# The last 16 rows of each head gathered in one transfer of 48 rows instead of three of 16, under a new list of steps

## The chip, the cores and the metric

One core of a Trainium2 chip runs the whole program. Its engines are TensorE (PE, matmuls; its weight loads are listed as PEld), VectorE (DVE), ScalarE (ACT), GpSimd (POOL) and SyncE (SP). Each works through its own queue in order. All transfers of this kernel are issued from SP's queue. The metric is device time in microseconds (us): the median of the runs before is 541.8 us, of three runs from 539.09 to 542.12.

## The reference

Two stages follow each other. The first is a gated linear recurrence for 4 batches and 8 heads over 768 steps, with head size 48:

```python
for t in range(S):
    state = alpha[:, :, t, :, None] * state + einsum('bhd,bhe->bhde', k[:, :, t], v[:, :, t])
    y[:, :, t] = einsum('bhd,bhde->bhe', q[:, :, t], state)
```

The second takes the 3072 tokens of width 384 that result through two layers with 2048 hidden units: `h = x @ w_in`, `g = h * erf(softplus(h))`, `out = g @ w_out`. All of it is float32.

## The kernel before, in words

The 768 steps are cut into 12 chunks of 64. For a chunk `n` the program has these steps, each a method of `Chunk`: `la`, `lk`, `lq`, `lv` load alpha, K, Q and v; `a1` makes the running product A of alpha (DVE); `ln` and `ex` its inverse (ACT); `w1`, `w2`, `w3` scale K with it and `a3` scales Q with A (DVE); `kx` and `qx` gather (below); `t` transposes K, `s` multiplies K by Q, `u` multiplies K by v into the state T, `q` multiplies Q by the old state and `y` adds the part from within the chunk (all PE), with copies on ACT or DVE behind them.

The second stage has 16 weight tiles for each layer. They arrive as 64-bit numbers and are turned into float32 and split into a high and a low half by the steps `wi_f` and `wo_f` (a load into `wst`, then six instructions on ACT and DVE). For chunk `n` the hidden units are done in four groups: `H_n_g_half` (first matmul, line 549; chunk 0 uses line 538 and the unsplit weights), `U`, `L1`, `G` (ACT tables and curves), `L2`, `Z` (DVE), `O_n_g` (split, then second matmul, line 617), and `out`.

**Layout and gather.** A head has 48 rows. Four head pairs stand in the tiles K and Q. Two halves of 64 partitions hold one head each, so that partitions 48 to 63 of each half would be empty. The fourth pair's 48 rows are loaded there: 16 of them behind each of the three first pairs (`KT` = 3). Before `s` and `q` can use the fourth pair, `last` (line 233) moves those 3 times 16 rows to 48 partitions of slot `KT`, in SBUF, for both halves. `kx` does it for K behind `w3`, `qx` for Q behind `a3`, and `ends` for the chunk's last column of A after every fourth chunk. Chunk 0 does its loads and products in two pieces (pairs 0 and 1, then the rest), and its gathers too.

**Order.** A written list, `SCHED`, of 1642 steps fixes the order on PE, ACT, DVE and SP: `steps()` takes the words one by one, and each engine gets its instructions in that order. A word `x` that stands several times is the step's next part each time; the prefix `v:` puts its copy on DVE instead of ACT. POOL holds a few small fills: the tail of `kn` in `t`, and a `token` behind each part of `q`, for which `y` waits. Large tiles share one pool of 24 buffers. In the compiled program each transfer waits on one of eight counters in turn, thus for the transfer issued eight before it.

Of the kernel before, what the change touches and what calls it, by code (L numbers as in the profile page):

```python
# [44 lines left out]
wi_15 wi_2 wi_7 wi_13 H_0_1_0 wi_15 wi_14 wi_3 v:wi_0 w2_2 lk_2 wi_13 wi_4 wi_12 wi_9 wi_15 wi_14 v:wi_12 wi_8 s_1
wi_3 s_1 wi_10 s_1 wi_2 wi_4 wi_1 H_0_0_1 w3_2 lv_1 H_0_0_1 H_0_2_0 wi_0 H_0_1_1 wo_9 wi_1 U_0_1 q_1 wo_7 wi_15 wi_0
t_1 wi_12 wi_1 wi_13 wo_9 v:wo_9 wi_12 v:wi_14 wo_7 wi_13 H_0_0_0 H_0_0_0 y_1 y_1 wi_0 wi_10 u_1 wi_3 wi_10 y_1 wi_11
wi_11 lq_2 wi_14 a3_2 wi_14 wi_6 wi_10 u_1 wo_9 H_0_2_0 wi_14 kx_2 v:y_1 U_0_0 la_3 v:wi_9 wo_2 H_0_3_1 wo_2 v:wo_2
a1_3 y_1 wo_9 L1_0_1 wo_13 t_2 wi_15 wi_13 wi_13 wo_1 wo_15 qx_2 wi_12 v:wi_11 wo_15 wo_0 v:wo_15 wi_14 H_0_3_1 y_1
H_0_3_0 wo_9 H_1_1_0 wi_11 s_2 wo_1 v:wo_1 t_2 wo_0 wi_12 lq_3 ln_3 wi_0 q_2 q_2 wi_11 wo_13 wo_3 t_2 wo_9 wo_15  # L50
H_1_1_0 wo_2 wo_2 wo_5 s_2 H_0_2_1 H_1_3_0 s_2 wi_11 wi_11 wo_15 wo_3 wo_1 v:wo_0 wi_9 wo_4 wi_10 wi_10 wi_15 H_0_2_1
wo_0 lv_2 ex_3 wo_15 w1_3 wo_15 v:wo_7 H_1_1_1 wo_7 H_1_3_0 wo_5 w2_3 H_1_0_1 wo_7 L1_0_1 wo_0 L1_0_0 H_1_1_0 y_2 wo_1
v:wo_3 u_2 wo_3 H_0_3_0 wo_0 y_2 a3_3 lk_3 w3_3 wo_4 wo_11 H_1_3_0 wo_7 wo_6 wo_13 v:wo_11 wo_1 L1_0_0 u_2 v:wo_4
H_1_2_1 lv_3 y_2 wo_13 H_1_0_0 y_2 H_2_0_0 wo_2 H_2_0_1 v:wo_11 H_1_1_1 L1_0_0 y_2 qx_3 L1_0_1 wo_13 wo_6 v:wo_6 wo_1
H_1_1_1 y_2 kx_3 U_0_3 wo_11 wo_4 H_1_0_1 L2_0_1 G_0_1 H_2_0_1 H_1_0_0 wo_2 wo_7 H_1_0_1 wo_3 wo_3 H_1_2_0 H_1_2_1
H_1_0_0 la_4 H_1_2_0 wo_4 H_2_0_0 L2_0_0 L2_0_0 G_0_0 L2_0_1 wo_0 H_2_0_0 H_1_2_1 wo_6 wo_13 H_1_2_0 q_3 la_6 H_2_0_1
v:wo_4 wo_3 s_3 s_3 s_3 Z_0_0 wo_4 Z_0_1 t_3 t_3 t_3 H_2_1_0 U_0_2 v:wo_5 wo_11 wo_5 q_3 L1_0_3 wo_14 u_3 gd_3 L1_0_3
wo_10 H_2_1_1 lq_4 y_3 wo_11 Z_0_0 O_0_0 H_1_3_1 u_3 H_2_2_1 wo_13 wo_6 wo_6 a1_4 H_1_3_1 H_2_2_1 L1_0_2 wo_11 H_2_2_1
ends_3 L1_0_3 wo_8 O_0_0 H_2_1_0 L1_0_2 y_3 y_3 y_3 wo_5 wo_10 H_2_2_0 L1_0_2 ln_4 Z_0_1 L2_0_3 L2_0_3 y_3 v:wo_8
# [10 lines left out]
Z_1_3 v:out_0_1 U_2_3 O_1_2 U_2_2 O_1_2 out_0_1 U_2_1 L1_2_1 H_3_3_0 qx_5 H_4_0_1 O_1_2 H_4_0_1 v:H_3_3_0 O_1_2  # L70
out_0_0 H_4_0_0 O_1_2 w3_5 H_4_2_1 L2_2_0 O_1_3 L1_2_1 H_4_2_0 L1_2_3 L1_2_1 v:H_4_0_1 H_3_3_1 kx_5 Z_2_0 L1_2_2 O_1_2
Z_2_0 t_5 t_5 t_5 O_1_3 q_5 q_5 H_3_3_1 O_1_3 v:H_4_0_0 lv_5 a1_6 H_3_3_1 s_5 L2_2_1 L2_2_1 O_2_0 L1_2_3 G_2_1 u_5 s_5
s_5 u_5 O_1_3 O_2_0 O_2_0 a1_7 L1_2_3 O_1_3 L1_2_2 y_5 y_5 O_2_0 y_5 Z_2_1 L1_3_0 O_1_3 L2_2_3 v:y_5 O_2_0 L1_2_2 ln_6
H_5_1_0 L1_3_1 Z_2_1 lk_6 O_2_0 ex_6 O_2_1 G_2_3 y_5 y_5 gd_6 L2_2_3 L2_2_2 O_2_1 H_4_3_0 G_2_2 w1_6 L2_2_2 O_2_1
Z_2_2 out_1_0 Z_2_3 Z_2_2 U_4_0 H_4_3_0 v:O_2_2 O_2_1 H_5_1_0 lq_6 H_4_1_0 L1_3_0 H_5_1_1 L1_3_0 H_4_3_1 out_1_0
H_5_1_1 out_1_1 out_1_1 w2_6 L2_3_0 L1_3_1 L1_3_1 H_4_1_0 H_5_1_1 w3_6 O_2_1 H_4_1_1 kx_6 O_2_1 L2_3_1 lv_6 a3_6 qx_6
H_4_3_1 v:H_5_1_0 L2_3_0 L1_4_0 H_4_1_0 G_3_1 O_2_2 O_2_2 v:H_4_3_0 v:H_4_3_1 H_4_1_1 H_4_1_1 gd_7 O_2_2 U_4_2 t_6
v:t_6 t_6 s_6 G_3_0 U_3_2 U_4_1 u_6 q_6 Z_2_3 O_2_2 O_2_3 s_6 H_5_2_1 Z_3_0 s_6 Z_3_0 U_3_3 q_6 L2_3_1 Z_3_1 L1_3_2
O_2_3 L1_4_1 O_2_2 L1_4_1 u_6 H_5_0_1 O_2_3 H_5_0_1 L1_4_0 O_2_3 L1_4_1 Z_3_1 H_5_0_1 O_3_1 y_6 y_6 y_6 y_6 L1_3_3
# [832 lines left out]
```

## Time and profile before

| | |
|---|---|
| median of 3 runs | 541.8 us (539.09 to 542.12) |
| profiled execution | 541.78 us, span 540.0 us |
| PE busy | 497.8 us |
| DVE busy | 467.5 us |
| ACT busy | 461.5 us |
| mean granted TensorE clock | 0.979 |
| transfers by `last` (line 236) | 72 for K, 72 for Q, 12 for `ends` |

The busy time counts instructions that overlap once. PE runs for 92% of the span, so the time is PE's work plus the places where PE stands still or runs at a lower clock; most of the reading is to find those places and what ended each.

### The profile page before, as it was taken

Reading aid. Unit: us, or ns where it says so; the run is one execution under the profiler, and the core shown is the slowest. Engines: PE = TensorE matmul, PEld = TensorE weight load, DVE = VectorE, ACT = ScalarE, POOL = GpSimd, SP = SyncE. Lnnn points to the kernel's source line nnn. Section 1 sums busy time; section 2 is a strip of 40 time slices with the busy share of each in tenths; the row PEclk is TensorE's granted clock in tenths of the full one; section 3 lists DMA queues with packets and bytes.
Section 4 is the critical chain, followed back from the end, with each engine's and each line's share of the span. In section 5 each row is a group of like instructions: output and inputs, shape, how many; then the busy total and the mean of one; then the engine's idle time right before and its main releaser. Section 6 shows DMA issues by size and latency. Waiting matters only on the chain.

```text
span 540.0 us, 17857 instructions
## 1 busy us (share of the span) xinstructions
PE 497.8 (92%) x7892; PEld 480.3 (89%) x7892; DVE 467.5 (87%) x567; ACT 461.5 (85%) x589; POOL 6.2 (1%) x48
## 2 busy tenths in 40 slices
...
## 3 DMA queue, kind: packets, MB, share of 16 engines
...
## 4 chain that ended last, share of the span: by engine, by line
PE 69%; ACT 8%; DMA 8%; DVE 7%; issue 3%; SPq 3%; ACTq 0%; DVEq 0%
PE acc L617 33%; PE ph L549 27%; PE py L456 5%; DMA wst<-in_moe_w_in_dram 4%; ACT w L205 2%; SPq L236 2%; PE pu L409 2%; DMA wst<-in_moe_w_out_dram 2%; PE pS L363 1%; ACT s L205 1%; DVE A L303 1%; ACT L204 1%; PE pn L383 1%; DVE w L581 1%; DMA Q<-in_qk_dram 1%
## 5 line engine op out<-in xcount | busy, mean ns | idle before, releaser
L617 PE MATMUL acc<-gh,wo_hi 128*128 128x256 f32 x576 | 137.4, 279 | 0.9 <-ACT gh L211 0.9
L617 PE MATMUL acc<-gh,wo_lo 128*128 128x256 f32 x576 | 136.9, 279 | 0.0
L549 PE MATMUL ph<-x_hi,wi_hi 128*128 128x256 f32 x528 | 127.9, 283 | 1.0 <-ACT x_hi L211 0.4
L549 PE MATMUL ph<-x_hi,wi_lo 128*128 128x256 f32 x528 | 126.0, 279 | 0.6 <-issue 0.4
L617 PEld LDWEIGHTS acc<-gh,wo_hi 128*128 128x128 f32 x576 | 109.2, 190 | 1.6 <-ACT gh L211 1.1
L617 PEld LDWEIGHTS acc<-gh,wo_lo 128*128 128x128 f32 x576 | 109.2, 190 | 0.0
L549 PEld LDWEIGHTS ph<-x_hi,wi_hi 128*128 128x128 f32 x528 | 100.1, 190 | 3.5 <-issue 1.2
L205 ACT ACTIVATE s<-s 128x1024 f32<-128x1024 f32 x96 | 99.5, 1053 | 3.6 <-DVE t L579 3.1
L549 PEld LDWEIGHTS ph<-x_hi,wi_lo 128*128 128x128 f32 x528 | 100.2, 190 | 0.3 <-issue 0.2
L617 PE MATMUL acc<-gl,wo_hi 128*128 128x256 f32 x576 | 80.2, 280 | 3.4 <-issue 3.4
L617 PEld LDWEIGHTS acc<-gl,wo_hi 128*128 128x128 f32 x576 | 72.2, 189 | 4.6 <-issue 3.8
L549 PE MATMUL ph<-x_lo,wi_hi 128*128 128x256 f32 x528 | 72.5, 280 | 0.0
L549 PEld LDWEIGHTS ph<-x_lo,wi_hi 128*128 128x128 f32 x528 | 66.1, 190 | 0.2
L204 ACT ACT_TABLE_LOAD x50 | 64.2, 1283 | 1.7 <-PEq L862 0.8
L579 DVE TENSOR_TENSOR t<-s,w 128x1024 f32<-128x1024 f32 x48 | 58.1, 1219 | 6.3 <-ACT w L205 3.3
L590 DVE TENSOR_TENSOR s<-s,w 128x1024 f32<-128x1024 f32 x48 | 58.2, 1220 | 2.9 <-ACT s L205 2.0
L603 DVE TENSOR_TENSOR gl<-hs,gh 128x1024 fp32r<-128x1024 f32 x48 | 58.2, 1219 | 0.7 <-ACT gh L211 0.4
L592 DVE SCALAR_TENSOR_TENSOR hs<-s,hs 128x1024 f32<-128x1024 f32 x48 | 58.3, 1220 | 0.5
L581 DVE SCALAR_TENSOR_TENSOR w<-t,w 128x1024 f32<-128x1024 f32 x48 | 58.1, 1220 | 0.4
L205 ACT ACTIVATE s<-hs 128x1024 f32<-128x1024 f32 x48 | 49.6, 1053 | 6.3 <-DVE hs L213 3.2
L205 ACT ACTIVATE w<-s 128x1024 f32<-128x1024 f32 x48 | 50.1, 1052 | 5.7 <-DVE w L581 2.6
L205 ACT ACTIVATE w<-w 128x1024 f32<-128x1024 f32 x48 | 50.0, 1054 | 0.6
...
## 6 DMA issues: line engine op xcount, KB each, us to landing
...
```

Source lines behind the costliest of these rows:

```text
L204: nc.scalar.preload_act_table_set(table)
L205: nc.scalar.activation(*args, **kw)
L236: nc.sync.dma_start(out=out[r0 + kt : r0 + D : KT], in_=in_[r0 + D : r0 + HD, kt])
L409: nc.tensor.matmul(out=pu[i][half * HD : (half + 1) * HD, z : z + D], lhsT=keys, rhs=self.vv[toks, m, h * HD : h * HD + D], start=True, st ...
L456: nc.tensor.matmul(out=self.py[i][c0 : c0 + 32, kt, m, :], lhsT=left[r0 : r0 + rows, l0 : l0 + 32], rhs=right[r0 : r0 + rows], start=kt == ...
L549: nc.tensor.matmul(out=ph[:, u * self.TB : (u + 1) * self.TB].rearrange("p (a t) -> p a t", t=CT), lhsT=wt[:, kt, fs], rhs=xt[:, at, kt], ...
L579: nc.vector.tensor_tensor(out=t, in0=s, in1=w, op=ALU.mult)
L581: nc.vector.scalar_tensor_tensor(out=w, in0=t, scalar=2.0, in1=w, op0=ALU.add, op1=ALU.mult)
L590: nc.vector.tensor_tensor(out=s, in0=s, in1=w, op=ALU.mult)
L592: nc.vector.scalar_tensor_tensor(out=h, in0=s, scalar=RT2 / 2, in1=h, op0=ALU.subtract, op1=ALU.mult)
L603: nc.vector.tensor_tensor(out=gl, in0=h, in1=gh.bitcast(F32), op=ALU.subtract)
L617: nc.tensor.matmul(out=self.acc[dm // n][:, dm % n * self.TB : (dm % n + 1) * self.TB], lhsT=wt[:, f, dm * P : (dm + 1) * P], rhs=gt[:, c0 ...
```

## The change

`last` issues one transfer for each half: 48 partitions are written from 16 partitions with three rows each. The rows and where they go are the same. `gather` in chunk 0 moves all of it in its second part and nothing in its first. A gather is 2 transfers where it was 6 (4 and 2 in chunk 0's two parts); the 26 gathers have 52 transfers where they had 156. `SCHED` is another list of the same 1642 steps, in another order, with 93 words that have `v:` where there were 94.

```diff
 SCHED = """
...
-qx_4 Z_0_2 U_1_1 H_2_3_0 H_2_3_0 H_3_0_1 wo_10 wo_8 H_2_3_1 w3_4 kx_4 H_2_1_1 U_1_0 O_0_1 wo_12 H_2_1_0 la_5 Z_0_3
-H_3_0_0 L1_1_0 H_3_0_1 u_3 O_0_1 wo_10 H_3_1_1 q_4 v:wo_12 s_4 Z_0_2 v:H_3_0_1 q_4 wo_14 s_4 L1_1_0 L1_1_0 wo_12 t_4
...
+w3_4 G_0_2 L2_0_3 O_0_1 H_3_3_1 H_2_2_0 H_2_3_1 wo_12 H_3_1_0 L2_0_2 Z_0_2 H_2_3_1 wo_13 wo_13 O_0_0 H_3_1_0 H_3_1_0
+wo_12 U_1_2 O_0_1 Z_0_3 H_2_1_0 U_1_1 O_0_1 t_4 q_4 H_2_3_1 Z_0_2 U_1_0 O_0_1 wo_13 q_4 L1_1_2 v:t_4 kx_4 s_4 Z_0_3
...
-    def last(out, in_, kts=slice(0, KT)):
-        for kt in range(KT)[kts]:
-            for r0 in (0, HD):
-                nc.sync.dma_start(out=out[r0 + kt : r0 + D : KT], in_=in_[r0 + D : r0 + HD, kt])
+    def last(out, in_):
+        for r0 in (0, HD):
+            nc.sync.dma_start(out=out[r0 : r0 + D], in_=in_[r0 + D : r0 + HD])
...
         def gather(self, z):
             for ms in self.pieces():
-                last(z[:, KT].rearrange("p m i t -> p (m i t)"), z.rearrange("p a m i t -> p a (m i t)"), ms)
+                if ms.stop == KT:
+                    last(z[:, KT].rearrange("p m i t -> p (m i t)"), z[:, :KT].rearrange("p a m i t -> p a (m i t)"))
                 yield
...
-            last(ends[:, KT].rearrange("p m i -> p (m i)"), ends.rearrange("p a m i -> p a (m i)"))
+            last(ends[:, KT].rearrange("p m i -> p (m i)"), ends[:, :KT].rearrange("p a m i -> p a (m i)"))
```

**SP at the start**, before: from the first gather to the weight loads behind the second pair of gathers. A, Q, K and raw_v are a chunk's inputs, wst a weight tile; `Q<-Q` and `K<-K` are gathers.

```order
L236 DMA Q<-Q 16x256 x4
L287 DMA raw_v<-in_v_dram 128x1024
L236 DMA Q<-Q 16x256 x2
L236 DMA K<-K 16x256 x6
L653 DMA wst<-in_moe_w_in_dram 128x768 x3
L267 DMA K<-in_qk_dram 128x768
L653 DMA wst<-in_moe_w_in_dram 128x768 x2
L267 DMA Q<-in_qk_dram 128x768
L653 DMA wst<-in_moe_w_in_dram 128x768 x4
L236 DMA K<-K 16x256 x6
L236 DMA Q<-Q 16x256 x6
L653 DMA wst<-in_moe_w_in_dram 128x768 x5
```

The same engine in the change, from the last input load ahead of the weights to the third gather:

```order
L266 DMA K<-in_qk_dram 128x768
L653 DMA wst<-in_moe_w_in_dram 128x768
L235 DMA Q<-Q 48x1x256 x2
L653 DMA wst<-in_moe_w_in_dram 128x768
L235 DMA K<-K 48x1x256 x2
L653 DMA wst<-in_moe_w_in_dram 128x768 x3
L235 DMA Q<-Q 48x1x256 x2
L653 DMA wst<-in_moe_w_in_dram 128x768
```

Nine weight loads stood behind 12 short transfers and ahead of 12 more; now 2 to 4 short ones stand between the weight loads. The first weight load is the tenth transfer of the program and was the fifth.

**SP at chunk 4**, before, from the last load ahead of the gathers to the one behind them:

```order
L267 DMA K<-in_qk_dram 128x768
L236 DMA ends<-ends 16x4 x6
L236 DMA Q<-Q 16x256 x6
L236 DMA K<-K 16x256 x6
L251 DMA A<-in_alpha_dram 128x780
```

In the change:

```order
L235 DMA ends<-ends 48x1x4 x2
L266 DMA Q<-in_qk_dram 128x768
L266 DMA K<-in_qk_dram 128x768
L250 DMA A<-in_alpha_dram 128x780
L653 DMA wst<-in_moe_w_out_dram 128x768
L235 DMA Q<-Q 48x1x256 x2
L235 DMA K<-K 48x1x256 x2
L287 DMA raw_v<-in_v_dram 128x1024
```

Eighteen short transfers in a row have become six, and four loads stand between `ends` and the two others.

**PE where the most small matmuls stand together**, before (chunks 10 and 11, with `y` of chunk 10 behind 12 large matmuls that are not shown):

```order
L549 MATMUL ph<-x_lo,wi_hi 128x256 x12
L383 MATMUL pn<-ident,K 128x128 x6
L363 MATMUL pS<-Q,K 64x64 x64
L409 MATMUL pu<-raw_v,kn 64x48 x32
L549 MATMUL ph<-x_hi,wi_hi 128x256
```

In the change, such a place is at chunk 7 (`y` of chunk 7 follows 18 large matmuls later):

```order
L617 MATMUL acc<-gh,wo_lo 128x256
L383 MATMUL pn<-ident,K 128x128 x6
L456 MATMUL py<-Q,T 32x64 x32
L363 MATMUL pS<-Q,K 64x64 x32
L409 MATMUL pu<-raw_v,kn 64x48 x32
L549 MATMUL ph<-x_hi,wi_hi 128x256
```

The products K by Q of chunks 10 and 11 are no longer one block of 64; at chunk 7 the transposes, two kinds of products and the state's product now follow each other.

## Rows read from the trace of the kernel before

**Rows 1.** Page, part 1: busy us (share of the span) and instructions.
```profile
PE 497.8 (92%) x7892; PEld 480.3 (89%) x7892; DVE 467.5 (87%) x567; ACT 461.5 (85%) x589; POOL 6.2 (1%) x48
```

**Rows 2.** Windows: stretch, its length, busy of each engine, granted clock, DMA share, GB/s.
```profile
0.00:20.00 20.00, 7.00 (x144) 5.63 (x144) 12.65 (x20) 8.90 (x18) 3.19 (x17) 1.00 0.62 207
20.00:40.00 20.00, 16.60 (x285) 13.80 (x286) 14.56 (x27) 13.60 (x29) 0.09 (x1) 0.91 0.73 254
60.00:120.00 60.00, 58.81 (x1148) 55.97 (x1147) 58.47 (x92) 58.93 (x100) 0.59 (x6) 1.00 0.41 129
```

**Rows 3.** Windows, a stretch within the second pair of gathers.
```profile
30.00:32.00 2.00, 2.00 (x11) 1.82 (x10) 1.97 (x5) 2.00 (x5) 0.00 (x0) 1.00 0.07 17
```

**Rows 4.** Timeline of SP's queue, start to 34 us: start, us, line, transfers.
```profile
6.71 2.51 SPq L236 DMA_DIRECT2D Q<-Q  x4
11.17 3.69 SPq L236 DMA_DIRECT2D K<-K  x6
23.91 4.83 SPq L236 DMA_DIRECT2D K<-K  x6
29.34 4.08 SPq L236 DMA_DIRECT2D Q<-Q  x6
```

**Rows 5.** Waits: engine and line, releaser, us in total, times, longest.
```profile
ACT wst L211 <- DMA wst<-in_moe_w_in_dram: 10.6, 5, 4.0
DVE wst L660 <- DMA wst<-in_moe_w_in_dram: 5.2, 3, 3.1
```

**Rows 6.** Line 236 (gathers) and 653 (weight loads): issue ns min/median/max; landing of line 236.
```profile
L236 SPq DMA_DIRECT2D K<-K x72: 506/587/1862, 11.2 to 395.9; - x72
DMA to landing us min/median/max: 1.7/2.0/6.6
L653 SPq DMA_DIRECT2D wst<-in_moe_w_out_dram x16: 327/328/1516, 38.7 to 111.5; - x16
```

**Rows 7.** Timeline of SP's queue at chunk 4.
```profile
112.42 4.45 SPq L236 DMA_DIRECT2D ends<-ends  x6
116.92 3.75 SPq L236 DMA_DIRECT2D Q<-Q  x6
120.77 3.70 SPq L236 DMA_DIRECT2D K<-K  x6
```

**Rows 8.** Chain of waits there: start, us, what.
```profile
118.37 0.95 DVE K L342
...
123.87 3.67 DMA K<-K
```

**Rows 9.** Windows around PE's three longest losses behind the start.
```profile
124.00:132.00 8.00, 5.46 (x142) 5.01 (x143) 3.87 (x9) 3.41 (x5) 0.29 (x3) 0.79 0.42 124
214.00:222.00 8.00, 5.37 (x165) 4.93 (x158) 3.76 (x6) 4.97 (x6) 0.09 (x1) 0.79 0.23 74
402.00:412.00 10.00, 6.61 (x139) 6.29 (x120) 5.04 (x7) 7.35 (x9) 0.00 (x0) 0.66 0.22 74
```

**Rows 10.** Timeline of SP's queue and DVE at chunk 6, and PE's wait there.
```profile
208.48 0.95 DVE L348 TENSOR_TENSOR Q<-Q,A 128x768 f32<-128x768 f32 x1
212.04 3.67 SPq L236 DMA_DIRECT2D Q<-Q  x6
216.52 0.29 PE L363 MATMUL pS<-Q,K 48*64 48x64 f32 x2 [2.42 <-DMA Q<-Q]
```

**Rows 11.** Timeline: PE behind its three gaps without a releaser, a load.
```profile
274.74 1.42 PE L617 MATMUL acc<-gl,wo_hi 128*128 128x256 f32 x10 [1.61 <-issue]
348.14 2.10 PE L617 MATMUL acc<-gl,wo_hi 128*128 128x256 f32 x17 [1.75 <-issue]
406.47 0.44 PE L456 MATMUL py<-sT,raw_v 64*32 64x64 f32 x9 [3.39 <-issue]
399.80 0.34 SPq L287 DMA_DIRECT2D raw_v<-in_v_dram  x1
```

**Rows 12.** Chain of waits, a piece of PE work: start, us, what.
```profile
277.51 1.36 PE ph L549 x12
```

More of the change, by code (lines that the diff above doesn't have):

```diff
@@ L45 @@
[L45 to L59, printed above, removed]
@@ L70 @@
[L70 to L79, printed above, removed]
@@ new lines @@
+wi_10 wi_5 v:wi_5 wi_8 ln_3 wi_6 wi_7 wi_4 wi_15 ex_3 t_2 wi_14 wi_3 wi_5 wi_10 gd_3 wi_6 wi_12 kx_2 wi_5 v:wi_10
+wi_14 qx_2 wi_11 wi_11 q_1 t_2 wi_6 H_0_1_1 H_0_0_1 wi_3 s_1 wi_4 wi_5 lv_1 H_0_1_0 wo_7 wi_10 s_1 y_1 wi_13 wi_10
+lv_2 wi_15 U_0_0 u_1 wi_11 w1_3 wi_6 v:wi_14 wi_11 v:wi_11 wi_9 wi_1 wi_4 wo_5 wi_5 wi_8 v:wi_8 u_1 y_1 H_0_2_1
+v:H_0_1_0 y_1 y_1 wi_14 H_0_1_1 U_0_1 lk_3 w2_3 wi_14 wi_8 L1_0_0 ends_3 wi_12 wi_11 u_2 wi_9 v:wi_9 s_2 v:wi_12 wi_15
+H_0_3_1 y_1 s_2 wo_8 H_1_1_1 H_1_0_1 wi_1 s_2 y_1 wo_7 wo_15 wi_14 v:wo_7 wi_9 wi_9 wi_8 q_2 w3_3 kx_3 wi_12 wo_7
@@ new lines @@
+wi_13 wo_4 v:wo_4 H_1_2_1 qx_3 wo_10 Z_0_1 wo_10 wo_9 v:wo_9 v:wo_3 H_0_3_0 H_1_2_0 H_1_1_1 Z_0_0 wo_11 v:wo_10
+H_1_2_1 wo_0 lv_3 wo_1 wo_6 H_2_0_1 wo_10 t_3 U_0_3 H_2_2_0 wo_4 s_3 wo_2 wo_1 s_3 v:wo_9 wo_11 q_3 H_2_2_0 H_1_3_1
+s_3 ends_3 wo_12 wo_3 U_0_2 L1_0_2 wo_9 H_2_3_0 q_3 wo_0 lq_4 wo_4 a1_4 wo_2 L1_0_3 H_2_3_0 wo_6 H_1_3_1 H_1_3_1
+H_1_3_0 wo_3 wo_1 v:H_2_3_0 y_3 v:wo_12 v:wo_11 H_1_3_0 y_3 u_3 y_3 y_3 wo_4 O_0_0 wo_12 wo_10 wo_10 wo_5 lk_4 u_3 y_3
+H_2_0_0 H_3_3_0 v:wo_6 wo_11 H_2_1_1 la_5 wo_9 wo_9 y_3 wo_10 wo_3 wo_6 wo_4 L1_0_2 H_1_3_0 O_0_0 O_0_0 wo_13 wo_9
@@ new lines @@
+H_2_1_1 ln_4 H_3_3_0 wo_3 O_0_0 L1_0_3 H_2_1_1 wo_5 ex_4 H_2_1_0 wo_6 wo_6 wo_11 wo_11 v:H_3_3_0 a3_4 H_2_0_0 w1_4
+wo_11 H_3_3_1 qx_4 L1_0_3 L2_0_3 H_2_0_0 L1_0_2 G_0_3 w2_4 wo_6 H_2_1_0 wo_13 gd_4 O_0_0 H_2_0_1 u_3 H_3_3_1 L2_0_2
+w3_4 G_0_2 L2_0_3 O_0_1 H_3_3_1 H_2_2_0 H_2_3_1 wo_12 H_3_1_0 L2_0_2 Z_0_2 H_2_3_1 wo_13 wo_13 O_0_0 H_3_1_0 H_3_1_0
+wo_12 U_1_2 O_0_1 Z_0_3 H_2_1_0 U_1_1 O_0_1 t_4 q_4 H_2_3_1 Z_0_2 U_1_0 O_0_1 wo_13 q_4 L1_1_2 v:t_4 kx_4 s_4 Z_0_3
+O_0_1 s_4 t_4 wo_13 wo_13 lv_4 wo_12 H_2_2_1 O_0_2 O_0_2 L1_1_0 O_0_1 H_2_2_1 H_3_1_1 H_2_2_1 O_0_3 L1_1_0 s_4 a1_5
@@ new lines @@
+L1_1_0 O_0_3 O_0_2 L1_1_2 y_4 u_4 wo_14 wo_14 y_4 L2_1_0 O_0_2 v:y_4 y_4 H_4_3_1 y_4 y_4 u_4 O_0_2 L2_1_0 L1_1_1
+L1_1_1 L1_1_1 L2_1_1 H_4_3_0 L1_1_2 L2_1_2 wo_14 wo_14 G_1_0 Z_1_0 Z_1_0 U_2_0 wo_14 G_1_2 H_4_3_1 L2_1_2 H_3_1_1
+H_4_2_0 O_0_2 v:H_3_1_1 U_1_3 Z_1_2 v:wo_14 U_2_1 wo_14 O_1_0 lk_5 H_4_2_0 G_1_1 H_4_2_0 H_4_3_0 L2_1_1 H_4_3_0
+H_4_2_1 Z_1_1 O_1_0 Z_1_1 Z_1_2 ln_5 O_0_3 O_1_0 L1_2_1 la_6 gd_2 lq_5 H_4_0_1 O_1_0 O_0_3 H_3_2_1 ex_5 O_0_3 H_4_3_1
+L1_2_0 L1_1_3 gd_5 L1_2_0 L1_1_3 v:O_1_1 O_1_0 w1_5 w2_5 w3_5 L1_2_1 O_0_3 O_1_1 a3_5 out_0_1 O_1_0 L1_1_3 L2_1_3
@@ new lines @@
+out_0_1 H_3_0_0 L1_2_0 O_1_1 L1_2_1 O_1_2 L2_2_0 H_4_0_1 qx_5 H_4_0_0 L2_2_1 la_9 O_1_1 L2_2_0 H_4_2_1 L2_1_3 G_1_3
+H_4_2_1 O_1_1 O_1_2 H_3_2_1 U_2_3 H_4_0_0 lk_6 O_1_1 Z_1_3 G_2_0 H_3_0_0 H_3_0_0 kx_5 O_1_2 U_2_2 H_3_2_0 H_4_0_0
+H_4_0_1 L2_2_1 out_0_0 O_1_2 Z_1_3 q_5 Z_2_0 s_5 Z_2_0 s_5 G_2_1 L1_2_2 a1_6 q_5 O_1_2 Z_2_1 O_1_3 L1_2_2 out_0_0
+L1_2_2 H_3_0_1 s_5 O_1_2 Z_2_1 lv_5 lq_6 ln_6 H_3_0_1 O_1_3 O_1_3 L1_2_3 ex_6 H_3_2_0 H_3_2_0 w1_6 O_1_3 L1_2_3 t_5
+H_3_2_1 v:H_3_0_1 a3_6 v:t_5 t_5 y_5 O_2_0 w2_6 y_5 u_5 u_5 O_1_3 L2_2_2 H_4_1_0 y_5 v:y_5 U_3_0 O_2_1 la_7 w3_6 U_4_0
@@ new lines @@
+G_2_2 L1_2_3 y_5 L2_2_2 O_2_0 O_2_0 y_5 O_1_3 out_1_0 out_1_1 t_6 t_6 O_2_0 H_4_1_0 O_2_0 v:t_6 L1_3_0 L1_3_0 qx_6 q_6
+Z_2_2 kx_6 Z_2_2 s_6 L1_3_0 H_4_1_0 s_6 s_6 L1_4_0 q_6 H_5_3_1 O_2_0 H_5_3_1 U_3_1 L2_2_3 L2_2_3 G_2_3 O_2_1 O_2_1
+out_1_0 L2_3_0 H_4_1_1 U_4_2 O_2_1 H_4_1_1 Z_2_3 G_3_0 Z_2_3 lv_6 U_3_3 a1_7 y_6 u_6 u_6 L1_3_3 y_6 L2_3_0 v:y_6 y_6
+v:H_5_3_1 Z_3_0 y_6 O_2_1 out_1_1 L1_3_1 L1_3_1 L1_3_1 O_2_2 H_5_1_0 L1_3_3 L1_3_3 H_5_2_0 U_3_2 Z_3_0 O_2_1 H_5_1_1
+y_6 O_2_3 O_2_2 O_2_2 H_5_2_0 v:H_4_1_1 v:O_3_0 L2_3_1 L2_3_1 G_3_1 O_2_2 O_3_0 L1_3_2 L1_3_2 H_5_1_1 O_3_0 L2_3_3
@@ new lines @@
+L1_6_1 Z_5_1 qx_9 O_5_1 w1_9 H_7_0_1 H_7_0_0 w2_9 w3_9 O_4_3 out_4_1 out_4_1 G_5_2 O_5_1 H_7_3_1 kx_9 O_5_0 U_6_3
+H_7_1_0 O_5_1 H_7_1_0 Z_5_2 Z_6_0 H_7_0_0 H_7_0_0 gd_8 v:H_7_1_0 L2_6_1 out_4_0 O_5_1 Z_5_2 L2_6_1 t_9 s_9 ln_10
+out_4_0 O_5_1 v:t_9 lq_10 lv_9 la_11 v:H_7_2_1 H_8_1_0 H_7_2_0 v:O_5_2 O_5_1 H_8_1_0 G_6_1 s_9 H_7_2_0 s_9 t_9 q_9
+O_6_0 Z_6_1 Z_6_1 u_9 L1_6_3 L1_6_3 v:H_7_2_0 q_9 H_8_1_1 H_8_1_0 L1_6_2 O_5_2 O_5_2 u_9 ex_10 L1_6_3 O_6_0 O_6_0
+L1_6_2 L1_6_2 L2_6_2 H_8_1_1 U_7_2 G_6_2 H_8_2_1 y_9 v:H_8_1_1 L2_6_3 y_9 y_9 O_5_2 O_6_0 U_7_3 y_9 G_6_3 L2_6_2 y_9
@@ new lines @@
+L2_6_3 Z_6_3 a3_10 y_9 O_5_2 w1_10 O_6_0 U_7_0 H_9_0_0 O_6_0 a1_11 O_6_1 U_7_1 O_5_3 L1_7_3 L1_7_3 O_5_2 H_9_0_0
+L1_7_2 L1_7_1 L1_7_1 Z_6_3 O_5_3 H_8_0_0 L1_7_1 H_8_2_1 O_5_3 L1_7_3 H_8_3_0 O_5_3 w2_10 Z_6_2 Z_6_2 L1_7_0 L1_7_0
+L1_7_2 O_6_1 O_6_1 L1_7_2 O_5_3 lk_10 w3_10 H_8_2_1 O_6_1 O_5_3 O_6_1 H_8_3_0 L2_7_3 L2_7_3 L1_7_0 H_9_0_0 out_5_1
+O_6_1 kx_10 L2_7_1 G_7_1 H_9_0_1 G_7_3 v:O_6_2 O_6_2 O_6_2 H_8_3_0 H_9_0_1 H_9_0_1 O_6_2 L2_7_0 L2_7_1 G_7_0 Z_7_1
+out_5_0 qx_10 H_8_0_0 L2_7_0 H_8_0_1 O_6_2 H_8_2_0 O_6_2 U_8_1 L2_7_2 H_8_0_1 out_5_1 Z_7_0 Z_7_0 O_6_3 H_8_0_0
```

115 lines of the change are left out of this document (51 added, 64 removed).

## The prediction

> **What bounds the kernel now.** I began with the page's busy times: PE works for 497.8 us of a span of 540.0, DVE and ACT for about 465 each [rows 1]. So the time is PE's work, which the change leaves as it is, plus the places where PE is late or slow. The windows show where they are. In the first 20 us PE is busy for 7.0, in the next 20 for 16.6, and DVE for 12.7 and 14.6; from 60 to 120 us all three engines are busy for 58 to 59 of 60 [rows 2]. What is lost at the start is therefore not made up later. Behind the start I looked for windows with a lower granted clock, and three stand out: around 124, 214 and 402 us [rows 9]. The waits and the chain then say who ended each of these gaps.
>
> At the start, SP's queue is the cause. Its gathers at 6.7 to 15 us and at 23.9 to 33.4 us stand between the weight loads [rows 4], and in the middle of the second pair the transfer engines are 7% busy [rows 3]. ACT then waits 10.6 us in five places for weights to land and DVE 5.2 us in three [rows 5]. At 124 us the chain itself runs through a gather: K of chunk 4 is scaled at 118.37 + 0.95 = 119.3 us, but six transfers for `ends` and six for Q stand ahead on SP, the six for K are issued from 120.77 to 124.5, and the last lands at 123.87 + 3.67 = 127.5 [rows 7, 8]. From scaled K to the product: 8.2 us. At 214 us it is Q of chunk 6: scaled by 209.4, issued from 212.0 behind K's gather, and PE waits 2.42 us for it [rows 10]. The gap near 402 us is of another kind: nothing releases PE after 3.39 us, and the same holds for two of 1.61 and 1.75 [rows 11].
>
> **The issue.** A gather transfer takes SP 0.587 us to issue, median of 72, and 2.0 us to land; a weight load, with 128 rows of three times the length, takes 0.328 [rows 6]. No row shows 48 rows written from 16. Below, its issue is bounded by 0.33 (the larger load costs no more) and above by 3 x 0.587 = 1.76 (if rows set the price). I take 0.59: a load with eight times the rows costs less than a gather, so rows are not what is paid for. Landing: between 2.0, the median, and 3.67, the slowest of the rows I read. A gather then needs 2 x 0.59 + 2.0 to 3.67 = 3.2 to 4.9 us, and 4.4 to 6.0 behind another gather. On SP, 26 x 4 = 104 issues x 0.59 = 61 us go; SP limits nothing in total, so this counts only where a wait ends on it.
>
> **The sum, part by part.**
>
> Start. Four gathers come ahead of or among the first ten weight loads, 24 transfers that become 8: 16 x 0.59 = 9.4 us less on SP. The gain can't be more than what DVE waited for weights, 5.2 us, because DVE is then the engine in demand; below it is nothing, because the new list starts the first weight load as the tenth transfer instead of the fifth. I take 3, nearer to the upper end, since DVE has the scans and scalings of three chunks to do until then.
>
> Chunk 4. In 124 to 132 us PE is idle for 8 - 5.46 = 2.5 us, and the granted clock of 0.79 costs 0.21 x 8 = 1.7 more: part of the window ran at the lower level, 1.2 GHz, after PE had stood still. Together 4.2. Between the words `w3_4` and `s_4` the list had 42 large matmuls for PE and now has 66 (at 1.36 us for 12 [rows 12], 4.8 and 7.5 us), beside the transposes and another part of `q`. The gather needs at most 6.0. I take the whole 4.2; nothing is the other end.
>
> Chunk 6. From 214 to 222: 8 - 5.37 = 2.6 idle and 1.7 of clock, 4.3. Between `a3_6` and the first product that uses Q there were 36 large matmuls, 4.1 us; now 60, 6.8 us, and `y_5` and `u_5` besides. I take 4.3 of 0 to 4.3.
>
> The rest of the gathers cost nothing on PE, before or after: other work covers them. If the cover of one went, it would cost what chunk 4 cost. The Trainium skill, "DMA: Bandwidth & Descriptors", section "Rules for kernel authors", says to issue a transfer early and wait for it late, since its fixed cost then overlaps with compute; by that rule a shorter gather is worth nothing where it is early enough. The trace agrees for most gathers and not for those two.
>
> The gaps without a releaser. The one near 402 us costs 3.4 idle and 0.34 x 10 = 3.4 of clock, 6.8; with 1.6 and 1.75 there are 10.2 us. The longest comes where 64 products K by Q, 32 for the state and 64 for `y` pass PE in a few microseconds while a load of v, issued at 399.80, is on its way. The new list parts chunks 10 and 11 but packs chunk 7 as densely, with loads of v, K and alpha near. I take no net change; all could go (-10.2) or as many come again (+10.2).
>
> ACT and DVE: the number of table loads that the list asks for stays at 50, and some two copies' worth of work moves from DVE to ACT. Nothing for PE.
>
> Sum: 541.8 - 3 - 4.2 - 4.3 = 530.3. The profiled execution, 541.78, is also the median of the runs, so nothing is to be shifted. Next in line is PE itself, with those gaps and the last 10 us of stores.
>
> **The rivals.**
>
> *Hidden, or not shorter.* If the issue costs 1.76, a gather takes SP 3.5 us as before; or DVE and ACT, 98% busy from 60 to 120 us, hold PE at the pace they had, and the two gaps move elsewhere. For it: most gathers wait for nobody. Against it: two named waits, in a place with more cover now. With half of one gap gone: 541.8 - 2 = 540.
>
> *Slower, by gaps without a releaser.* A dense block of small matmuls during a load stops PE for some 3.4 us, and the clock falls: 6.8 each [rows 9, 11]. The place is chunk 7's block. It decides from the third such gap more than before: 541.8 - 11.5 + 3 x 6.8 = 551. For it: three such gaps exist, and the list was ordered anew. Against it: the new list has one block as dense as the old one's, not three. The Trainium skill, "Runtime: NRT & Kernel Launch", section "Instruction fetch mechanics", says that an engine streams its program in blocks through its own DMA queue and that crossing a block is mostly hidden; by it these gaps would not be the program's fetch and a dense block would be safe. The trace does not agree that PE runs on without a gap there.
>
> *More than the gathers.* The new list also avoids the longest such gap and some of the small ones: 530.3 - 9 = 521.
>
> **The numbers.** The forecast, 530 with its own range of 525 to 536 (the start at 0 or 5.2, a small gap more or less), has 0.54; hidden 0.26, at 537 to 545; slower 0.10; more 0.10. 1% of the median, about what can be told from no change here, is 5.4 us: faster means under 536.4, slower over 547.2. Faster: 0.54 + 0.10, less the forecast's upper edge, gives 0.63; slower 0.11; the rest, 0.26, is within 1%. The range of 520 to 544 leaves out slower, and the outer edges of the hidden and the best case.
>
> **What would show it.** In the new profile a gather pair should take SP some 1.2 us; transfer engines should not fall under a tenth of their time between 28 and 34 us; DVE's waits for weights should be under 3 us; products K by Q of chunks 4 and 6 should not wait for a gather, and the granted clock should stay at 1.0 there. If the issue of one transfer is over 1.2 us, the first rival holds. If the waits go and the time stays, DVE and ACT set PE's pace. If two or more gaps of over 3 us without a releaser stand in PE's rows, the second rival is at work.

## The result and the profile after

| | before | changed |
|---|---|---|
| median | 541.25 us (539.09 to 542.12, 4 runs) | 517.56 us (515.06 to 520.20, 4 runs) |
| ratio | | 0.9569, 95% interval 0.9505 to 0.9632 |
| profiled execution | 541.78 us, span 540.0 | 519.14 us, span 517.1 |
| mean granted clock | 0.979 | 0.988 |

The change gains 23.7 us; the forecast's sum had 11.5. The page of the changed kernel, parts 1 and 2 (engine busy times, then slices of 12.9 us in tenths):

```profile
PE 487.5 (94%) x7892; PEld 471.8 (91%) x7892; DVE 466.3 (90%) x562; ACT 463.5 (90%) x594; POOL 6.1 (1%) x48
...
PE   0879999999999999999999999999999999999993
...
PEclk9979999999999999999999999999999999999997
DMA  8894464202113311113312114010321000000003
```

Against [rows 1], PE's busy time itself is 10.3 us shorter for the same 7892 matmuls. The mean granted clock, 0.988 in place of 0.979, stands for some 4.5 us of that (an estimate: 0.009 of 498 us); what the rest is, no run shows. The idle time fell from 42.2 to 29.6 us. Between the third slice and the last the row of PE has no digit under 9. The windows that answer to [rows 2, 3, 9], with the same columns:

```profile
0.00:20.00 20.00, 7.24 (x150) 6.08 (x150) 15.12 (x24) 12.16 (x26) 3.08 (x16) 1.00 0.83 282
20.00:40.00 20.00, 15.48 (x350) 12.64 (x351) 19.21 (x36) 17.20 (x37) 0.31 (x4) 0.84 0.95 332
30.00:32.00 2.00, 1.77 (x97) 1.54 (x97) 2.00 (x2) 1.24 (x4) 0.00 (x0) 1.00 1.03 377
124.00:132.00 8.00, 8.00 (x237) 7.64 (x236) 7.55 (x9) 7.12 (x9) 0.00 (x0) 1.00 0.10 39
214.00:222.00 8.00, 8.00 (x73) 8.00 (x72) 7.34 (x8) 7.95 (x10) 0.00 (x0) 1.00 0.18 51
402.00:412.00 10.00, 10.00 (x261) 9.36 (x263) 8.21 (x9) 9.46 (x12) 0.18 (x2) 1.00 0.01 3
```

DVE does 34.3 us of work in the first 40 us where it did 27.2; the transfer engines are nearly full from 20 to 40 us (0.95), and 30 to 32 us went from 7% to 100%. PE's three long losses are gone, and the granted clock there is 1.0. From 20 to 40 us the clock is lower than it was, 0.84 against 0.91. SP's queue at the start, answering to [rows 4] (start, us, line, transfers):

```profile
7.29 1.34 SPq L235 DMA_DIRECT2D Q<-Q  x2
...
11.99 1.20 SPq L235 DMA_DIRECT2D K<-K  x2
13.24 1.54 SPq L653 DMA_DIRECT2D wst<-in_moe_w_in_dram  x3
...
23.55 1.21 SPq L235 DMA_DIRECT2D K<-K  x2
24.92 4.17 SPq L653 DMA_DIRECT2D wst<-in_moe_w_in_dram  x4
```

The gather line, answering to [rows 6] (issue ns min/median/max, then landing in us):

```profile
L235 SPq DMA_DIRECT2D K<-K x24: 567/573/1412, 12.0 to 398.3; - x24
...
DMA to landing us min/median/max: 2.1/2.9/7.6
```

A transfer of 48 rows costs SP what one of 16 cost, 0.573 against 0.587 us, and lands in 2.9 instead of 2.0. DVE's waits for weights, 5.2 us in [rows 5], are gone from the list. Of the waits of PE for a gather only 0.2 us is left. One gap without a releaser of 3.02 us is new, at 35.48 us; it comes up again below.

### The profile page after: what moved, and what is told of

It is laid out like the page before. It is cut to its first block, busy times and chain, and to the rows that moved or that the text cites. A ratio compares the mean times of both kernels' runs of the same rounds, so it can differ in the third digit from the quotient of the medians.

```text
span 517.1 us, 17673 instructions
## 1 busy us (share of the span) xinstructions
PE 487.5 (94%) x7892; PEld 471.8 (91%) x7892; DVE 466.3 (90%) x562; ACT 463.5 (90%) x594; POOL 6.1 (1%) x48
## 3 DMA queue, kind: packets, MB, share of 16 engines
q8 instruction: 64, 1.05, 0.9%
## 4 chain that ended last, share of the span: by engine, by line
PE 88%; DVE 4%; DMA 3%; ACT 2%; issue 2%; SPq 0%; DVEq 0%
PE acc L617 38%; PE ph L549 33%; PE py L456 7%; PE pu L409 3%; PE ph L538 3%; PE pS L363 2%; DMA K<-K 1%; PE pn L383 1%; DMA Q<-in_qk_dram 1%; DMA raw_v<-in_v_dram 1%; DVE A L303 1%; DVE rw L330 1%; ACT hs L211 0%; DVE t L579 0%; ACT wst L211 0%
## 5 line engine op out<-in xcount | busy, mean ns | idle before, releaser
L617 PE MATMUL acc<-gl,wo_hi 128*128 128x256 f32 x576 | 77.9, 279 | 0.0
L617 PEld LDWEIGHTS acc<-gl,wo_hi 128*128 128x128 f32 x576 | 71.0, 188 | 0.5
```

What stands on the lines that cost most here:

```text
L617: nc.tensor.matmul(out=self.acc[dm // n][:, dm % n * self.TB : (dm % n + 1) * self.TB], lhsT=wt[:, f, dm * P : (dm + 1) * P], rhs=gt[:, c0 ...
```

## Experiments

Each is compared with runs of the kernel before in its own job, whose medians were 541 to 546 us. Gains in us are 1 less the ratio, times that median.

### Code or list

**e1_code_only**, the one-transfer gather under the list of before:

```diff
 # against the changed kernel
-SCHED = the new list
+SCHED = the list of before
```

> The list of before with the one-transfer gather. Theory A (the forecast's: the six-transfer gathers caused the late weights at the start and PE's gaps at chunks 4 and 6): all of the forecast 11.5 us, 528 to 532 us, and no PE wait for a gather near 124 and 214 us, while PE's gap of 3.4 us without a releaser near 400 us stays. Theory B (the new list made the gain, the gather only allowed it): 537 to 541. Issue of one 48-row transfer 0.58 us, as the profile after has it.

522.95 us (519.19 to 525.64), ratio 0.9615 [0.9557, 0.9674]: 20.9 us, more than either theory had. No wait of PE for a gather is left in its trace.

**e2_list_only**, the new list with six transfers to a gather:

```diff
 # against the kernel before
-SCHED = the list of before
+SCHED = the new list
```

> The list of after with the gather of six transfers. Theory A: the start is as late as before or later, since the weights stand behind the same short transfers, and only the cover that the list gives chunks 4 and 6 helps: 530 to 535 us. Theory B: 517 to 522. If the two parts simply add: 541.3 - 23.7 + 11.5 = 529.

539.04 us (537.78 to 540.26), ratio 0.9934 [0.991, 0.9958]: 3.6 us, less than every case named. So the gather is nearly all of it. In the trace of e2 the products of chunks 4 and 6 wait for no gather either, as the forecast had it of the new list's cover; but two products of the start wait 3.05 and 3.08 us for K's gather, at 21.41 and 38.37 us. The shorter gather closes the gaps of chunks 4 and 6 under the old list too.

### Which gathers

Three kernels with the list of before, in which only some gathers are short:

```diff
 def gather(self, z):
     for ms in self.pieces():
-        last(z[:, KT]..., z..., ms)
+        if self.n not in SHORT:
+            last(z[:, KT]..., z..., ms)
+        elif ms.stop == KT:
+            once(z[:, KT]..., z[:, :KT]...)
```

**e3_chunks_4_6**, `SHORT` = (4, 6), and `ends` of chunk 3:

> Before, with the one-transfer gather for K and Q of chunks 4 and 6 and for the ends of chunk 3 alone. Theory A: both named gaps go with their clock, 4.2 + 4.3 = 8.5 us: 532 to 534 us. Rival (the gaps only move, because ACT and DVE hold PE): 539 to 542.

537.66 us (534.15 to 542.19, 10 runs), ratio 0.9905 [0.9864, 0.9946]: 5.2 us, less than the 8.5. In its trace PE is busy for all of 204 to 222 us, and no wait for the gathers of these chunks is left. But a gap without a releaser now stands behind the products of chunk 4, and such gaps make 11.2 us in this trace, where they made 8.8 before:

```profile
128.38 0.63 PE L559 MATMUL ph<-x_lo,wi_hi 128*128 128x256 f32 x4 [1.46 <-issue]
```

**e4_chunks_0_2**, `SHORT` = (0, 1, 2):

> Before, with the one-transfer gather in chunks 0, 1 and 2 alone. Theory A: 3 us at the start, up to 5.2: 536 to 538 us, with the gaps at chunks 4 and 6 still there. Rival (the weights are bound by the transfer engines, not by SP's issues): 540 to 542.

534.91 us (529.53 to 536.78), ratio 0.9826 [0.9773, 0.9879]: 9.4 us, with 6.6 to 12.3 by the interval. Even its lower end is over the 5.2 that the prediction called the most that the start could give. Windows of this kernel, to set beside [rows 2]:

```profile
0.00:20.00 20.00, 7.66 (x262) 6.32 (x262) 14.77 (x25) 11.71 (x24) 3.20 (x17) 0.93 0.80 274
20.00:40.00 20.00, 18.00 (x250) 15.29 (x251) 19.60 (x38) 17.81 (x38) 0.18 (x2) 0.81 0.88 314
```

And SP's queue at the second pair of gathers:

```profile
21.28 1.22 SPq L240 DMA_DIRECT2D K<-K  x2
24.75 1.21 SPq L240 DMA_DIRECT2D Q<-Q  x2
26.00 2.50 SPq L663 DMA_DIRECT2D wst<-in_moe_w_in_dram  x5
```

The same five loads in the kernel before:

```profile
33.46 2.48 SPq L653 DMA_DIRECT2D wst<-in_moe_w_in_dram  x5
```

They are issued 7.5 us earlier, and DVE does 34.4 us of work by 40 us, 7.2 more than before. Both lie within the interval of the time gained: the start is worth about the time by which SP's queue moves up, and more than the part of it that DVE spent on a wait that bears the weights' name.

**e6_rest**, `SHORT` = (3, 5, 7, 8, 9, 10, 11), and `ends` of chunk 7:

> The list of before; only the gathers of chunks 3, 5 and 7 to 11 and the ends of chunk 7 are one transfer per half, all others six as before. The prediction said that these cost nothing on PE because other work covers them: 541 us, no change. If the parts add up (all gathers gave 0.9615, chunks 0 to 2 gave 0.9826 and chunks 4 and 6 with one ends 0.9905), they are worth some 1.1%: about 535 us.

538.46 us (534.44 to 544.78, 10 runs), ratio 0.9889 [0.9844, 0.9934]: 6.0 us. The three ratios multiplied give 0.9624, and all gathers together 0.9615. The same kernel once more, **e17_rest_again**:

> The kernel whose gathers are short only in chunks 3, 5 and 7 to 11, once more, for a profile of a common execution: 535 to 540 us. If the later gathers held PE by the products, the same work is done some 1 us earlier after each of these chunks. If their gain is that PE's program is shorter by the waits for four transfers fewer at each gather, which moves the borders of its blocks, the steps stand at the gaps without a releaser (275, 348 and 406 us).

539.87 us (537.34 to 540.47, 3 runs), ratio 0.9975 [0.9787, 1.0164]. Its trace does not show where a gain would lie: the gaps without a releaser are still there, three of them 1.34, 0.77 and 3.69 us long, and from 20 to 40 us, where its gathers are as before, PE does 14.52 us of work against 16.60 [rows 2], so that a later start may hide what is gained behind it. That the later gathers are worth something is shown by the ten runs alone; by what, stays open.

### SP's time or the rows' arrival

**e5_spare**, e1 with four spare transfers behind each gather:

```diff
+def spare(out, in_):
+    for r0 in (0, HD):
+        for k in range(2):
+            cs = slice(k * 128, (k + 1) * 128)
+            nc.sync.dma_start(out=out[r0 + D : r0 + HD, cs], in_=in_[r0 + D : r0 + HD, k, cs])
```

> The list of before and the gather in one transfer per half; behind each gather for K or Q stand four more transfers of 16 rows by 128 elements, into rows that nothing reads (rows 48 to 63 of slot KT). So the rows of the fourth pair land as early as with the short gather, but SP issues as many transfers as before (six per gather; ends alone keeps two). Theory 1 (the gain of the one-transfer gather is SP's time: every load and gather behind it starts earlier): at 0.59 us each the spare transfers give back nearly all of the 21 us, so 536 to 543 us, with the weight loads of the start back near 33 us. Theory 2 (the gain is that the products get their rows sooner): the time stays at 522 to 527 us.

533.6 us (530.29 to 534.99), ratio 0.9846 [0.9788, 0.9903]: between the two theories. The trace parts them by place. SP at the five loads, the waits of DVE and ACT up to 60 us, and two windows, all of this kernel:

```profile
34.20 3.46 SPq L660 DMA_DIRECT2D wst<-in_moe_w_in_dram  x5
```

```profile
DVE wst L667 <- DMA wst<-in_moe_w_in_dram: 8.5, 3, 5.1
```

```profile
ACT wst L211 <- DMA wst<-in_moe_w_in_dram: 11.5, 6, 4.8
```

```profile
0.00:20.00 20.00, 6.34 (x144) 5.18 (x144) 12.65 (x20) 8.90 (x18) 3.20 (x17) 0.97 0.63 204
20.00:40.00 20.00, 14.00 (x282) 11.60 (x282) 13.42 (x26) 13.19 (x29) 0.09 (x1) 0.76 0.74 254
```

The start is as late as before, or later [rows 2, 5], though its rows come with the first two transfers of each six: what counts there is how many transfers stand in SP's queue. But 8.4 us of gain remain (5.3 to 11.5 by the interval), and the start does not hold them. In the kernel before PE waited for gathers in these lines, the first two of them at chunks 4 and 6, the last at the start:

```profile
PE pS L363 <- DMA Q<-Q: 2.6, 2, 2.4
PE pS L363 <- DMA K<-K: 2.5, 2, 2.2
...
PE py L456 <- DMA Q<-Q: 1.4, 1, 1.4
```

With spare transfers 1.4 of these 6.5 us are left. K's gather of chunk 4 starts when it did, at 120.62 us against 120.77 [rows 7], although `ends` has no spare transfers; its rows come with two transfers instead of six. So the start gains by SP's queue, and chunks 4 and 6 by rows that land sooner. The spare transfers carry half as many bytes as those they stand for; their issue, 0.587 us at the median, is the same.

### Gaps without a releaser: where they stand

The count of PE's matmuls and weight loads (the x of the first two columns) from the start up to the gaps at 400.54 and 406.47 us of the kernel before, by windows:

```profile
0.00:400.49 400.49, 369.39 (x6447) 353.30 (x6448) 355.23 (x452) 350.90 (x471) 6.01 (x46) 0.99 0.30 96
0.00:406.42 406.42, 371.92 (x6575) 355.56 (x6576) 355.41 (x452) 354.85 (x474) 6.01 (x46) 0.99 0.30 96
```

12895 and 13151, just 256 apart. Written as a multiple of 256 and a rest, most gaps of all traces have a rest that falls slowly with the count (in the changed kernel 181 behind 2 x 256, 143 behind 33 and 126 behind 50; in all traces 95 to 126 behind 49 to 53), as it would if PE's queue also held a few instructions that the trace does not count. The theory: PE's program arrives in blocks of 256 instructions, and PE stands when it has used one up before the next is there. The test: put spare matmuls at the very start, which moves every border by as many instructions and should move nothing else.

```diff
 # e7, e8: in t of chunk 0, ahead of its transposes, N = 112 and 64
+for _ in range(N):
+    nc.tensor.matmul(out=pn[0][:HD, :HD], lhsT=ident[:, :HD], rhs=ident[:, :HD], start=True, stop=True)
```

**e7_before_p112:**

> The kernel before, with 112 spare 64x64 products ahead of chunk 0's transposes, where PE has nothing to do yet; nothing else is moved. In six traces the gaps without a releaser stand at counts of PE's matmuls and weight loads that differ by multiples of 256, less about 1.8 for each 256 since the start. Theory 1 (PE's program comes in blocks of 256 instructions, and PE stands where one was used up in under some 3.3 us while transfers were in flight): 224 instructions more ahead of them shift the borders to where no block of this list takes PE less than 3.3 us, so the gaps at 274, 348 and 406 us (6.8 us idle) shrink to under 2 us together and the lower clock behind the last goes: about 533 us. Theory 2 (a dense run of small matmuls stops PE during a load, wherever borders are): the 3.4 us stay where they are, 541 us.

540.58 us (534.30 to 544.53, 10 runs), ratio 0.9952 [0.9906, 0.9998].

**e8_after_p64:**

> The changed kernel, with 64 spare 64x64 products ahead of chunk 0's transposes, where PE has nothing to do yet; nothing else is moved. Theory 1 (blocks of 256 instructions): borders move by half a block, and 15 blocks between 20 and 372 us would then be used up in 1.5 to 2.9 us of PE's work, where four were before; short of 3.3 us each that is 17 us, less where no transfer is in flight, and the clock may fall behind some: 525 to 540 us, with many gaps without a releaser at the chunks' small matmuls. Theory 2 (dense runs, wherever borders are): the gaps stay as they are, 517 to 519 us.

526.58 us (524.35 to 528.54), ratio 0.972 [0.9654, 0.9785].

Both were mis-dosed. Each spare product left two matmuls and two weight loads in the trace, 0.222 us each, so that e7 moved the borders by 448 instructions, one block and three quarters, and e8 by 256: by nothing that would show. In e7 the gaps without a releaser fell from 8.8 to 5.1 us, but its spare products ran until 17.6 us, and chunk 0's transposes began at 17.50 instead of 9.84 us, so its time decides nothing. The 9 us that e8 lost go with the spare products' own time, from 13.2 to 23.0 us ahead of chunk 0's transposes. By accident it is the control. PE behind its gap in the changed kernel, and in e8 (line 458 is 456 there):

```profile
31.75 0.71 PE L456 MATMUL py<-Q,T 48*32 48x64 f32 x47
35.48 0.47 PE L456 MATMUL py<-Q,T 48*32 48x64 f32 x17 [3.02 <-issue]
```

```profile
41.09 0.71 PE L458 MATMUL py<-Q,T 48*32 48x64 f32 x47
43.86 0.47 PE L458 MATMUL py<-Q,T 48*32 48x64 f32 x17 [2.07 <-issue]
```

A whole block more ahead of it, and the gap is behind the same 47 of 64. Then the right doses, with a smaller product:

```diff
 # e9: N = 32; e10, e11, e12: N = 56; in s of chunk 0, ahead of its products
+for _ in range(N):
+    nc.tensor.matmul(out=ps[0][:HD, 0, :D], lhsT=ident[:HD, :HD], rhs=ident[:HD, :D], start=True, stop=True)
```

**e9_after_p32:**

> The changed kernel, with 32 spare small products (64x64 by 64x48) ahead of chunk 0's first products K by Q; nothing else is moved. Each leaves two matmuls and two weight loads in the trace, so this is 128 instructions, half a block of 256; they take PE about 1 us in all. (The 64 wider ones of the earlier run were 256 instructions, a whole block, and its gaps stood behind the same instructions as without them; they took PE 0.22 us each, twice.) Theory 1 (PE's program comes in blocks of 256): 15 blocks between 20 and 372 us are used up in 1.5 to 2.9 us of PE's work, and each of them for which transfers are in flight costs a gap of 0.5 to 3 us, some of the lower clock as well: 523 to 540 us. Theory 2 (dense runs during a load, wherever borders are): gaps behind the same instructions as in the changed kernel, 517 to 520 us.

531.01 us (525.05 to 533.55), ratio 0.9744 [0.9657, 0.9831]: 13 us over the changed kernel, 9.5 by the ratios, with some 15 us of gaps without a releaser in its trace in place of 6. Windows and PE at one count, first of the changed kernel, then of e9:

```profile
0.00:249.66 249.66, 230.91 (x4295) 219.58 (x4296) 232.99 (x318) 229.93 (x334) 5.04 (x37) 0.99 0.39 124
```

```profile
248.56 0.34 PE L456 MATMUL py<-sT,raw_v 64*32 64x64 f32 x15
249.71 1.35 PE L456 MATMUL py<-sT,raw_v 64*32 64x64 f32 x113 [0.81 <-issue]
```

```profile
0.00:258.14 258.14, 237.97 (x4295) 226.47 (x4296) 231.02 (x314) 229.09 (x331) 5.04 (x37) 0.98 0.38 119
```

```profile
255.17 0.88 PE L411 MATMUL pu<-raw_v,kn 64*64 64x48 f32 x33
258.19 1.11 PE L411 MATMUL pu<-raw_v,kn 64*64 64x48 f32 x31 [2.13 <-issue]
```

After the same 8591 instructions both stand, though one is amid `y` and the other amid `u`. A border decides where, not the work.

**e10_after_p56:**

> The changed kernel, with 56 spare small products there: 224 instructions. Theory 1: no block falls under 2.6 us of PE's work; the 3.0 us at 35 us (and the lower clock behind it) and the small gaps at 250 and 373 us go, with one or two of up to 1 us at 30 or 56 us in their place: 511 to 516 us. Theory 2: 517 to 520 us.

515.82 us (515.49 to 515.96), ratio 0.95 [0.9447, 0.9554]. The gaps at 250 and 373 us are gone; the same `y` of chunk 7 passes in one piece:

```profile
249.96 1.50 PE L458 MATMUL py<-sT,raw_v 64*32 64x64 f32 x128
```

But the gap at the start stayed, 2.79 us long and now behind 63 of those 64 products. By its ratio e10 can't be told from the changed kernel; but e9, in the same job and with fewer of the same spare products, took 15.2 us more.

**e11_before_p56:**

> The kernel before, with the same 56 spare small products: 224 instructions. Theory 1: every block takes PE 3.3 us or more, so the gaps of 1.6, 1.75 and 3.4 us go with the lower clock behind the last, some 10 us together, less what the spare products cost at the start: 531 to 537 us. Theory 2: 541 to 543 us.

543.56 us (541.64 to 544.75), ratio 1.0009 [0.9948, 1.0069].

**e12_code_p56:**

> The list of before with the one-transfer gather everywhere, and the same 56 spare small products. Without them this list is some 5 us behind the new one (522.95 against 517.56). If what the new list adds is that it avoids the longest gap at a block's border (3.2 us at 387 us, with the lower clock behind it), it is gone here: 514 to 518 us, level with the changed kernel. If the new list is better by other means (more work ahead of the gathers), 520 to 524 us.

525.94 us (525.22 to 527.52), ratio 0.9691 [0.9634, 0.9749].

In both traces the gaps without a releaser shrank as expected, from 8.8 to 3.0 us and from 7.4 to 2.7, and the times did not. The reason is in the edit: all spare products write one place, take 0.107 us each one after the other, and in these two kernels stand behind the transposes, from 11.2 to 23.7 us, where chunk 0's products wait for them. So these times don't decide. The same again with products that alternate between the quarters of the array, in front of all of PE's work:

```diff
 # e13, e14: in t of chunk 0; e15: in s of chunk 0, into ps; N = 56
+for k in range(N):
+    a, b = (slice(z * HD, (z + 1) * HD) for z in (k % 2, k // 2 % 2))
+    nc.tensor.matmul(out=pn[k % 2][b, :D], lhsT=ident[a, :HD], rhs=ident[a, :D], start=True, stop=True)
```

They run from 2.28 to 5.5 us, while PE has nothing to do. **e13_code_p56_early:**

> The list of before, the one-transfer gather everywhere, and 56 spare small products (224 instructions) ahead of chunk 0's transposes, spread over the four quarters of PE's array so that they take some 0.02 us each, between 2.3 us, when ident is ready, and 10 us, when PE gets its first work. Theory 1 (borders of blocks): the 7.4 us of gaps without a releaser of the same kernel without spare products fall to under 3 us, and the lower clock behind the one at 387 us goes: 513 to 517 us against 522.95. Theory 2 (the new list's gain over this one has other causes): 520 to 524 us.

516.62 us (513.28 to 519.02), ratio 0.9466 [0.9393, 0.9538]. The same list and gather without spare products had 0.9615. A window of e1, and the same of e13:

```profile
380.00:392.00 12.00, 8.84 (x191) 8.37 (x186) 8.00 (x12) 10.80 (x12) 0.00 (x0) 0.86 0.28 80
```

```profile
380.00:392.00 12.00, 11.47 (x280) 10.91 (x282) 9.44 (x14) 11.44 (x14) 0.00 (x0) 1.00 0.28 80
```

The gap of 3.16 us that e1 has at 387.30 is not there (one of 0.53 us is left at 385.69), and the clock stays at its upper level. By the medians e13 is 6.3 us under e1. Their ratios differ by more, but come from two jobs, and the changed kernel itself had 0.9569 in one job and 0.9461 in another (e16).

**e14_before_p56_early:**

> The kernel before with the same spare products at the same place. The earlier run lost 7.3 us at the start to them and was level with before at its end. Theory 1: without that loss it is 532 to 537 us. Theory 2 (what it gained later was only slack that the late start had left): 540 to 543 us.

541.62 us (536.24 to 548.35, 10 runs), ratio 0.992 [0.9871, 0.9969]: 4.4 us, about half of what theory 1 had. The time itself lies in the range of theory 2, in a job whose runs of the kernel before took 545.98 us, so that it does not decide between the two. A gap of 2.86 us at 407.83 us remains, where the model had a block of over 3.3 us; the model of block lengths is rough.

**e15_after_p56_early** and **e16_after_again**, the changed kernel as it is, in the same job:

> The changed kernel with 56 such spare products ahead of its first products, ended by 6 us instead of 14. The earlier run with the slow ones had 2.8 us of gaps without a releaser instead of 6.1, and 515.82 us. Theory 1: 512 to 516 us, 2 to 4 us under the changed kernel on the same chip. Theory 2: no difference, within 1 us.

> The changed kernel once more, on the same chip as the version with spare products: 515 to 520 us.

514.33 us (513.37 to 515.56), ratio 0.9422 [0.9378, 0.9466], and 515.82 us (514.75 to 520.39), ratio 0.9461 [0.9409, 0.9513]. The medians differ by 1.5 us and the intervals overlap: e15 may be the best version of this case, but that it beats the changed kernel is not shown.

The traces also time each packet of the queue that brings instructions (q8). In the kernel before, from 403.08 to 406.47 us, the gap of 3.39 us, the transfer engines were full for the first quarter, and one packet of q8 went through (40 slices in tenths; packets, MB):

```profile
DMA  9999999999653810000000000000000000000000
q8 instruction: 1, 0.02, 1.8%
```

It starts at 404.21 us and takes 0.96, and PE goes on 1.30 us after its end. The nineteen traces of this case have 81 gaps of 0.3 us or more without a releaser. 75 of them end 1.13 to 1.64 us after the end of such a packet of 16,384 bytes, though these packets come only every 8 us or so (64 of them in 517 us). The other six, among them the gaps of 2.0 us that remain in e12 and e13, stay unexplained.

## Why the prediction was wrong

The direction was right, and so was the mechanism at the start and at chunks 4 and 6; the size was half. By its own steps:

- **The issue** held: 0.573 us against the 0.59 taken, so that rows are not what is paid for. The landing of 2.9 us lies within its 2.0 to 3.67.
- **The start failed.** The step was "the gain can't be more than what DVE waited for weights, 5.2 us". The part was worth 9.4 us (e4). A wait list names who came last at each wait. In the kernel before DVE was idle for 12.8 of the first 40 us, and 3.4 of that bear the weights' name; K of chunk 1 was issued behind the same gathers, and 2.9 us were one wait for products of PE, which itself had stood 1.64 us without a releaser, up to 16.96 us:

```profile
DVE sT L373 <- PE pS L363: 2.9, 1, 2.9
```

  The term of 9.4 us less on SP, worked out in the same paragraph, was the better bound: the queue was the path, the five loads moved up by 7.5 us, and in e5 spare transfers alone put them back. That it equals the measured 9.4 is luck: the interval is 6.6 to 12.3, and e4 shortens six gathers, not four.
- **Chunks 4 and 6** were mis-sized the other way: 8.5 forecast, 5.2 measured (e3; 2.9 to 7.4 by the interval). The gaps closed as described, but taking their idle time and clock in full left no room for what PE then loses elsewhere: the gaps without a releaser are 2.4 us more in e3's trace. The rest of the difference stays open.
- **"The rest of the gathers cost nothing"** is not borne out by the ten runs of e6, 6.0 us (3.6 to 8.5); the three runs of e17 leave zero open. Multiplied, the parts agree with the whole (0.9624 and 0.9615) only with that share in it. No wait of PE in the trace of before names it.
- **The gaps without a releaser**, left at no net change, are the last part: e1 to the changed kernel is 5.4 us by the medians and 2.5 by the ratios, whose intervals overlap, and e13 shows that the old list gets as low (0.9466 against 0.9461, in one job) once its borders are moved. The new list has nothing beyond that which these runs could measure. The prediction read three such gaps where the trace has five; the others are 1.64 us, up to 16.96 us, and 0.41, up to 400.54. The rival "more than the gathers" had named this and given 521 us a chance of 0.10.
- **The rival "slower"** had the right ingredients, a dense run of small matmuls during a load, but not the condition: a border of the program must fall into it as well. e9 is that rival made real, 13 us for 128 instructions that moved the borders by half a block. The changed kernel's page has this line for the queue that brings instructions (packets, MB):

```profile
q8 instruction: 64, 1.05, 0.9%
```

1.05 MB in 64 packets are 16.4 KB each. The Trainium skill, "Runtime: NRT & Kernel Launch", section "Instruction fetch mechanics", states blocks of 16 KiB, or 256 instructions: the traces agree, with gaps 256 instructions apart. The Trainium skill, in the same section, also calls the cost of a border mostly hidden, and the prediction took that as a reason against this rival. The measurement decides otherwise: 3.39 us at one border before [rows 11], 0.41 to 1.75 at four more, and nothing of 0.3 us or more at the others. Moved borders move the gaps, and PE goes on when a block has come, so they are the program's fetch.

Sum of the parts as measured: 9.4 + 5.2 + 6.0 = 20.6 for the gather, where all gathers together gave 20.9, and 2.5 to 5.4 from e1 to the changed kernel, which moved borders give under the old list as well.
